# The y halves of a fused attention, expert and gated-MLP kernel: scaled in place, their sums and low halves on GpSimd, with the fetches of the dense weights in another place

## The chip, the cores and the metric

The kernel runs on one core of a Trainium2 chip. The metric is the device time of one execution in microseconds (us). The kernel before took 1469.22 us as the median of three runs (1468.58 to 1472.0). The execution that the profiler recorded took 1465.18 us, of which the trace spans 1463.4 us.

## The reference

Three stages follow one another on 4608 tokens of width 512:

```
attention, 8 x 8 heads, 576 tokens, 64 wide, 32 memory slots:
    a   = softmax(phi over tokens);  k_m = a^T k;  v_m = a^T v
    x   = softmax(q k_m^T / 8) v_m                     -> [4608, 512]
experts (8, capacity 576 each), from all gate logits sorted:
    out[tokens of e] = max(x[tokens of e] @ w1[e], 0) @ w2[e]
                       w1[e]: 512 x 1024, w2[e]: 1024 x 512
gated MLP:
    h   = out @ w_in                                   (512 x 2048)
    out = (h * clip(h + 3, 0, 6) / 6) @ w_out          (2048 x 512)
```

All of it is float32 for the caller. The kernel multiplies in pairs of 16-bit halves: a float32 tile is scaled by a power of two, its high half is the float16 rounding, its low half is the scaled tile minus the high half. A product then takes three matmuls (high by high, high by low, low by high).

## The kernel before, in words

**Stages.** Attention and routing take roughly the first 210 us. The tiles of x are then written to DRAM (`xd<-xs`, through SyncE's queue). From there the work goes by expert, k = 0 to 7. The tokens of an expert are gathered from `xd` by indirect DMAs that GpSimd issues (`h<-xd,ix` for expert 0, `xg<-xd,ix` for the others), transposed on TensorE (`xp`) and split into halves (`xt`). L1(k) is 192 matmuls `p<-xt,w` of 128x288, whose 16 results are taken out by ScalarE (`h<-p`) and VectorE; L2(k) is 192 matmuls `p<-h,w`, whose 8 results ScalarE writes to the y tiles (`y<-p`), with a maximum by VectorE (`ym<-y`).

**Weights.** `weights()` at L1026 runs over T = 0 to 15, where T = 2k is w1 and T = 2k+1 is w2 of expert k. For each it issues four indirect gathers on GpSimd (`wst<-in_moe_w_dram,ei`), squares each on ScalarE (`wscr<-wst`, with a sum), derives a scale (a small matmul `amx<-ident,s_..`, then VectorE), and converts in eight steps: the high halves on ScalarE (`w<-wst,s`), the low halves on VectorE, or for three of the eight on GpSimd while T is 1 to 3.

**The y split.** `ysplit(k)` at L1499 turns the output of expert k into seven pairs of halves, three of blocks of y and four of sums of blocks (a Strassen-like scheme). Before, VectorE makes the four sums and the seven low halves, and ScalarE the seven high halves; the scale `sy` is applied in each of the fourteen steps. A ninth split takes the tokens left over.

**The dense weights.** w_in and w_out are fetched in 32 blocks of 512 KB (`dst`), by SyncE's queue (`dload`, L1212; the fetch itself is at L74 and L76), and converted by VectorE, ScalarE and GpSimd (`cv`, `cva`, `wga`, `wgb`, `wo`), w_in by way of DRAM (`wid`, `ws`). `dense_max`, `dense`, `turn` and `dense_piece` (L1229 on) run this work.

**Units.** Nine units then multiply the split y by the dense weights (`pq`, `pr`), apply the gate (`h`, on ScalarE, VectorE and GpSimd) and multiply by w_out (`acc`). The sequence on TensorE is L1(0), L2(0), L1(1), L2(1), unit 0, unit 1, L1(2), L2(2), L1(3), L2(3), unit 2, and so on, to units 6, 7 and 8.

**What sets the order.** Every engine works through its own instructions in the order in which they were written. That order comes from a model of the clock that runs while the kernel is built: each engine has an object (`A_` ScalarE, `V_` VectorE, `G_` GpSimd) with a modelled time `.t`, and generators yield the modelled time, and the engine, at which they want to go on. `spawn(task, lim)` starts such a generator as a task of its own. On the chip only semaphores and the order in each engine's queue count; the modelled delays exist there only as positions in the queues. Nearly every instruction has one line in the profile, L568, that of the engine objects' call; matmuls are L622 and the transposes L627.

Of the kernel before, what the change touches and what calls it, by code (L numbers as in the profile page):

```python
# [12 lines left out]
AF = mybir.ActivationFunctionType  # L13
OP = mybir.AluOpType
# [5 lines left out]
def attn_moe_kernel(ctx: ExitStack, tc: tile.TileContext, q, k, v, phi, w_gate, w1, w2, w_in, w_out, out):  # L20
    nc = tc.nc
# [535 lines left out]
    CK = Clock()  # L557
# [53 lines left out]
    def spawn(gen, lim=0.0, first=False):  # L611
        t = [CK.now, lim, gen, None]
        CK.tasks.insert(0 if first else len(CK.tasks), t)
# [413 lines left out]
    def weights():  # L1027
        for T in range(2 * E):
            k, which = divmod(T, 2)
            while k not in EIX:  # L1030
                yield CK.now + 0.3
            for c in range(4):
                w_issue(T, c)
                yield CK.now + 0.8, G_
            while not XD[0]:
# [1 line left out]
            sq = rt.tile([128, 4], F32, name="wsq", bufs=2)  # L1037
            for c in range(4):
                st, ready = WST[T, c]
                yield ready, A_  # L1040
                scr = wk.tile([128, 1024], BF16, name="wscr")
                A_.activation(scr, st, AF.Square, accum_out=sq[:, c:c + 1])
                yield (CK.now + 3.0, A_) if k > 3 else A_.t + (0.3 if T else -0.1)
# [169 lines left out]
    def dload(which, j):  # L1213
        tag = spare(1)
        BUSY.add(tag)
        DN[0] += 1
        st = wk.tile([128, 1024], I32, name="dst", tag=tag)
        dense_fetch(st, 16 * which + j)
        return tag, st, dma(1.5)

    EM = []
# [6 lines left out]

    def dense_max():  # L1229
        yield from dense_scale(0)  # L1230
        while not GI[0]:
            yield CK.now + 0.5
        ld = {}
        for n in range(ND[0], 32):
            which, j = divmod(n, 16)
            for i in range(n, min(32, n + 2)):
                while i == n and i not in ld and not spare(1):
                    yield CK.now + 0.3
                if i not in ld and spare(1):
                    ld[i] = dload(*divmod(i, 16))  # L1240
            done, DLD[n], ready = ld[n]
            yield ready, V_
            dense_abs(V_, n)
            yield V_.t
            BUSY.remove(done)
            if j == 15:
                yield from dense_scale(which)
# [5 lines left out]
    WG, WA, WX, NWS, CUR = set(), {}, {}, [0], [0]  # L1253

    def dense():
        while not GI[0]:
            yield CK.now + 0.5
        for which, j in PO:
            while not (SDR[which] and spare(1)):
                yield CK.now + 0.2  # L1260
            spawn(dense_piece(which, j, *dload(which, j)), 0.1)
            yield CK.now

    TURN = [0.0]

    def turn():
        while CK.now < TURN[0] or V_.t > CK.now + 0.05:
            yield max(TURN[0], CK.now + 0.05)
        TURN[0] = CK.now + (1.15 if NB[0] == 4 else 0.85)

    def dense_piece(which, j, done, st, ready):
        yield ready, V_
# [101 lines left out]
    def x_tiles(n):  # L1374
        for _ in range(n):
            if XN[0] == 2 * NT:
                break
            t, g = divmod(XN[0], 2)
            XN[0] += 1
            if g == 0:  # L1380
                XC[:] = [[False]]
                XC.append(bank(XC[0]))
            x_mm(t, ps, XC[1], g)
            CK.now += 0.435
            if g:
                x_ev(t)
                A_.t = max(A_.t, CK.now) + 0.5
                XC[0][0] = True
                XDT[0] = dma(0.73, A_.t)
            XD[0] = XN[0] == 2 * NT  # L1390

    HT, HD, YS, YD = {}, {}, {}, {}
# [105 lines left out]
    def ysplit(k):  # L1498
# [36 lines left out]
            YD[k][0] += 1  # L1535
        else:
            V_.memset(iv[:, 3:4], 1.0)
        t1, t2 = ya[:, :, 0:256], ya[:, :, 256:512]
        u1, u2 = yb[:, :, 0:256], yb[:, :, 256:512]
        ST[k] = [slot(7 * (k % 2) + i, [128, 2, 2, 256], F16, f"st{i}_") for i in range(7)]  # L1540
        nl = [0]
        x1, x2 = (slot(14 + i, [128, 2, 256], F32, f"sx{i}_") for i in range(2))
        V_.tensor_tensor(x1, t2, u2, op=OP.add)
        r1 = V_.t + HOP
        yield V_.t + 0.5, V_
        V_.tensor_tensor(x2, x1, t1, op=OP.subtract)
        r2 = V_.t + HOP
        yield V_.t + 0.5, V_
        V_.tensor_tensor(t2, t1, t2, op=OP.subtract)
        r3 = V_.t + HOP  # L1550
        for i, src, r in ((A11, t1, 0.0), (A12, u1, 0.0), (A22, u2, 0.0), (S1Y, x1, r1), (S2Y, x2, r2), (S3Y, t2, r3),
                          (S4Y, x1, 0.0)):
            if i == S4Y:
                V_.tensor_tensor(x1, u1, x2, op=OP.subtract)
                r = V_.t + HOP
            yield (max(r, CK.now + (0.9 if k == 2 else 2.0)), A_) if k > 1 else (max(r, CK.now + 2.0 * k), A_)
            A_.activation(ST[k][i][:, 0], src, AF.Copy, scale=s)

            def low(t=ST[k][i], src=src):
                yield (A_.t + HOP, V_) if k > 1 else A_.t + HOP  # L1560
                V_.scalar_tensor_tensor(t[:, 1], src, s, t[:, 0], op0=OP.mult, op1=OP.subtract)
                nl[0] += 1
            spawn(low(), 0.8)
            while i in (S1Y, S4Y) and nl[0] < (4, 7)[i == S4Y]:
                yield CK.now + 0.1
        YR[k] = True

    INV, SY = {}, {}
# [232 lines left out]
```

## Time and profile before

| | |
|---|---|
| median of three runs | 1469.22 us |
| profiled execution | 1465.18 us |
| its span in the trace | 1463.4 us |
| TensorE matmul (PE) | 1335.5 us, 91% of the span |
| VectorE (DVE) | 949.7 us, 65% |
| ScalarE (ACT) | 818.9 us, 56% |
| GpSimd (POOL) | 484.6 us, 33% |

The busy times are sums over an execution whose stages differ. In the stretch from 326 to 480 us, which holds the conversion of the dense weights beside expert 1 and the first units, VectorE is busy for nine tenths of the time; from 1002 us on it is busy for less than half.

### The profile page before, as it was taken

The page shows a single profiled execution, that of the slowest core. Times are in us where ns is not written, and L with a number is a line of the kernel's source. Part 1 is how long each engine was busy: PE and PEld are TensorE (multiplying, and loading weights), DVE is VectorE, ACT ScalarE, POOL GpSimd, SP SyncE. Part 2 cuts the span into 40 slices and gives each one's busy share as a digit, 9 for nine tenths or more (in the row PEclk, how much of TensorE's full clock was granted, in tenths as well). Part 3 has the DMA queues.
Part 4 walks back from the last instruction along what each step waited for, and adds up shares of the span by engine and source line. Part 5 has one row for each costly group of instructions (what it writes and reads, how often), then busy time and mean ns, then how long its engine had stood idle before and what let it go on. Part 6 is the DMA issues. An engine that isn't in the chain of part 4 may idle for free.

```text
span 1463.4 us, 27894 instructions
## 1 busy us (share of the span) xinstructions
PE 1335.5 (91%) x11132; PEld 1001.6 (68%) x11132; DVE 949.7 (65%) x2232; ACT 818.9 (56%) x1560; POOL 484.6 (33%) x530
## 2 busy tenths in 40 slices
PE   4778886987999999989899999999999999999998
PEld 3667665866765667877568767876786687666664
DVE  4687975778898888885875687476246424435322
ACT  3667655468687455554654565465437524545543
POOL 5775312145353343302332323323212211232323
PEclk9989997899999999999999999999999999999999
DMA  9984487446773353313332333234223202243321
GB/s 296 309 273 144 158 263 247 145 142 240 248 236 150 109 183 109 104 60 113 109 133 88 119 105 134 91 109 147 81 66 119 101 30 75 81 144 116 107 99 54
DMA packets 83490, 206.29 MB, mean 141 GB/s; under 512 B 11040, under 2 KB 41760, under 8 KB 83360
## 3 DMA queue, kind: packets, MB, share of 16 engines
q1 hardware_dynamic: 68192, 151.55, 30.6%
q0 software_dynamic: 15168, 52.96, 11.1%
q8 instruction: 87, 1.43, 0.4%
q14 instruction: 43, 0.35, 0.1%
HBM read 177.23 MB, written 27.26 MB: 140 GB/s over the span
## 4 chain that ended last, share of the span: by engine, by line
PE 56%; DVE 6%; issue 5%; ACT 2%; DMA 1%; POOL 1%; POOLq 0%; SPq 0%; ACTq 0%
PE acc L622 21%; PE p L622 16%; PE pq L622 10%; PE pr L622 8%; DVE h L568 1%; ACT h L568 1%; DMA wst<-in_moe_w_dram,ei 1%; PE xp L627 1%; DVE w L568 1%; DVE B L568 0%; DVE C L568 0%; PE rtp L838 0%; POOL h L568 0%; DMA ws<-wid 0%; POOL out_dram L568 0%
## 5 line engine op out<-in xcount | busy, mean ns | idle before, releaser
L622 PE MATMUL acc<-wo,h 128*128 128x512 f16 x1728 | 425.0, 380 | 0.3 <-DVE wo L568 0.2
L622 PEld LDWEIGHTS <-w 128*128 128x128 f16 x3072 | 338.2, 122 | 70.8 <-DVE w L568 8.1
L622 PEld LDWEIGHTS <-ws 128*128 128x128 f16 x3024 | 292.2, 98 | 109.8 <-issue 24.4
L568 POOL TENSOR_TENSOR h<-h,h 128x512 f16<-128x512 f32 x144 | 176.6, 1232 | 425.1 <-ACT h L568 300.5
L622 PEld LDWEIGHTS <-h 128*128 128x128 f16 x1728 | 166.3, 98 | 138.7 <-issue 2.3
L622 PE MATMUL p<-h,w 128*128 128x288 f16 x1536 | 206.2, 290 | 10.9 <-DVE w L568 3.9
L622 PE MATMUL p<-xt,w 128*128 128x288 f16 x1536 | 209.3, 291 | 7.3 <-POOL w L568 2.2
L568 ACT ACTIVATE h<-h,half_c,inv 128x512 f32<-128x512 f32 x144 | 116.5, 811 | 175.4 <-DVE h L568 147.3
L568 DVE SCALAR_TENSOR_TENSOR h<-h,h 128x512 f32<-128x512 f32 x144 | 102.4, 713 | 69.8 <-ACT h L568 69.5
L568 ACT ACTIVATE h<-pq,swv 128x256 f32<-128x256 f32 x216 | 101.4, 470 | 63.7 <-PE pq L622 60.4
L568 POOL DMA_INDIRECT wst<-in_moe_w_dram,ei x64 | 65.2, 1018 | 190.7 <-ACT y L568 50.5
L568 ACT ACTIVATE h<-p 128x288 f16<-128x288 f32 x128 | 52.3, 409 | 127.5 <-PE p L622 126.0
L568 DVE SCALAR_TENSOR_TENSOR h<-pr,swv,h 128x256 f32<-128x256 f32 x144 | 69.1, 480 | 84.1 <-PE pr L622 78.1
L568 DVE SCALAR_TENSOR_TENSOR h<-p,h 128x288 f16<-128x288 f32 x128 | 57.5, 453 | 67.9 <-ACT h L568 64.6
L568 DVE SCALAR_TENSOR_TENSOR w<-wst,s,w 128x512 f16<-128x512 f32 x119 | 97.3, 825 | 1.1 <-ACT w L568 1.1
L568 ACT ACTIVATE h<-h 128x512 f16<-128x512 f32 x144 | 89.4, 621 | 8.3 <-DVE h L568 8.2
L568 ACT ACTIVATE w<-wst,s 128x512 f16<-128x512 f32 x119 | 82.7, 712 | 5.7 <-DVE s L568 5.7
L568 ACT ACTIVATE wscr<-wst 128x1024 bf16<-128x1024 f32 x64 | 67.4, 1053 | 15.3 <-DMA wst<-in_moe_w_dram,ei 14.9
L568 ACT ACTIVATE y<-p 128x288 f32<-128x288 f32 x64 | 25.5, 409 | 87.5 <-PE p L622 79.9
L568 DVE TENSOR_REDUCE ym<-y 128x1 f32<-128x288 f32 (+1 forms) x66 | 30.7, 472 | 62.0 <-ACT y L568 61.7
L568 POOL DMA_INDIRECT xg<-xd,ix x35 | 35.9, 1027 | 102.2 <-DVE ix L568 44.5
L568 POOL DMA_INDIRECT out_dram<-y,ix x36 | 36.7, 1019 | 83.1 <-ACT y L568 79.3
(550 smaller groups left out, 2194.3 us busy)
## 6 DMA issues: line engine op xcount, KB each, us to landing
ws<-wid SPq DMA_DIRECT2D x72, 896.0 KB, 4.6
dst<-in_moe_w_out_dram SPq DMA_DIRECT2D x28, 512.0 KB, 5.3
qt<-in_q_dram SPq DMA_DIRECT2D x8, 1024.0 KB, 13.2
dq<-in_moe_w_in_dram SPq DMA_DIRECT2D x16, 512.0 KB, 4.8
xd<-xs SPq DMA_DIRECT2D x32, 256.0 KB, 5.5
dst<-in_moe_w_in_dram SPq DMA_DIRECT2D x16, 512.0 KB, 4.3
kvt<-in_k_dram SPq DMA_DIRECT2D x7, 1152.0 KB, 11.3
kvt<-in_v_dram SPq DMA_DIRECT2D x7, 1152.0 KB, 12.4
```

The lines of the kernel that those rows point to most:

```text
L568: r = f(*a, **kw)
L622: nc.tensor.matmul(o, l, r, start=start, stop=stop, skip_group_check=more)
L627: nc.tensor.transpose(o, i, idn)
```

## The change

The change has four parts.

1. `ysplit`: VectorE first multiplies y by its scale, in place, in two instructions of 128x1024. The seven high halves stay on ScalarE, as copies without a scale. The four sums and the seven low halves go to GpSimd, as subtractions. Each pair of halves is a task of its own.
2. `dload`: three of the early dense blocks are fetched through GpSimd's queue, where before all were fetched through SyncE's. In the written order they stand behind the gathers of expert 0's tokens.
3. The dense work starts once expert 0's tokens have been asked for (`0 in XI`), where before it waited for a later mark (`GI`); in the stage with `NB == 4` its tasks may run further ahead (0.5 where 0.1 and 0.05 stood, and steps of 0.85 where 1.15 stood).
4. `weights`: the third gather waits in the model for x (`XD`), and for T = 1 to 3 the squares are put 2.5 modelled us later. The modelled landing of the last x tile is put 1.5 us later.

```diff
@@ weights()
             for c in range(4):
+                while c == 2 and not XD[0]:
+                    yield CK.now + 0.1
                 w_issue(T, c)
...
                 st, ready = WST[T, c]
-                yield ready, A_
+                yield ready + (2.5 if 0 < T < 4 else 0.0), A_
                 scr = wk.tile([128, 1024], BF16, name="wscr")
@@ dload()
-        dense_fetch(st, 16 * which + j)
+        dense_fetch(st, 16 * which + j, nc.gpsimd if NEM < DN[0] < NEM + 4 else nc.sync)
@@ dense_max(), dense()
-        while not GI[0]:
-            yield CK.now + 0.5
+        while 0 not in XI:
+            yield CK.now + 0.2
...
-            spawn(dense_piece(which, j, *dload(which, j)), 0.1)
+            spawn(dense_piece(which, j, *dload(which, j)), 0.5 if NB[0] == 4 else 0.1)
@@ turn()
-        while CK.now < TURN[0] or V_.t > CK.now + 0.05:
+        while CK.now < TURN[0] or V_.t > CK.now + (0.5 if NB[0] == 4 else 0.05):
             yield max(TURN[0], CK.now + 0.05)
-        TURN[0] = CK.now + (1.15 if NB[0] == 4 else 0.85)
+        TURN[0] = CK.now + 0.85
@@ x_tiles
-                XDT[0] = dma(0.73, A_.t)
+                XDT[0] = dma(0.73, A_.t) + 1.5
@@ ysplit()
+        for y in (ya, yb):
+            V_.tensor_scalar(y[:, :, 0:512], y[:, :, 0:512], s, None, op0=OP.mult)
+            V_.t -= 0.5
+            yield V_.t + 0.3, V_
...
-        V_.tensor_tensor(x1, t2, u2, op=OP.add)
...
-        V_.tensor_tensor(x2, x1, t1, op=OP.subtract)
...
-        V_.tensor_tensor(t2, t1, t2, op=OP.subtract)
...
-            if i == S4Y:
-                V_.tensor_tensor(x1, u1, x2, op=OP.subtract)
-                r = V_.t + HOP
-            yield (max(r, CK.now + (0.9 if k == 2 else 2.0)), A_) if k > 1 else (max(r, CK.now + 2.0 * k), A_)
-            A_.activation(ST[k][i][:, 0], src, AF.Copy, scale=s)
...
-                V_.scalar_tensor_tensor(t[:, 1], src, s, t[:, 0], op0=OP.mult, op1=OP.subtract)
...
+        def half(i, src, r):
+            yield r, A_
+            A_.activation(ST[k][i][:, 0], src, AF.Copy)
+            yield A_.t + HOP, G_
+            G_.tensor_tensor(ST[k][i][:, 1], src, ST[k][i][:, 0], op=OP.subtract)
+            nl.add(i)
+        r = V_.t + HOP
+        for i, src in ((A11, t1), (A12, u1), (A22, u2)):
+            spawn(half(i, src, r), 0.8)
+            yield CK.now + 0.7, G_
+        for i, o, p, q, op in ((S1Y, x1, t2, u2, OP.add), (S2Y, x2, x1, t1, OP.subtract), (S3Y, t2, t1, t2, OP.subtract),
+                               (S4Y, x1, u1, x2, OP.subtract)):
+            while i == S4Y and S1Y not in nl:
                 yield CK.now + 0.1
+            yield CK.now, G_
+            G_.tensor_tensor(o, p, q, op=op)
+            spawn(half(i, o, G_.t + HOP), 0.8)
+            yield G_.t, G_
+        while len(nl) < 7:
+            yield CK.now + 0.1
```

The model clock turns these edits into other orders on the engines. Three places matter for what follows.

**First place: the dense blocks beside expert 0's tokens.** On SyncE's queue before, the dense blocks (`dst`) stand directly behind the last writes of x (`xd`):

```order
L429 DMA xd<-xs_3441 128x512
L429 DMA xd<-xs_3455 128x512
L429 DMA xd<-xs_3469 128x512
L76 DMA dst<-in_moe_w_out_dram 128x1024 x2
L74 DMA dst<-in_moe_w_in_dram 128x4x256
L76 DMA dst<-in_moe_w_out_dram 128x1024 x3
```

On GpSimd's queue after the change, three blocks stand behind the five gathers of expert 0's tokens (`h<-xd,ix`):

```order
L568 DMA wst_3476<-in_moe_w_dram,ei_3356 128x1024
L568 DMA wst_3486<-in_moe_w_dram,ei_3356 128x1024
L568 DMA h_3507<-xd,ix_3499 128x512 x2
L568 DMA h_3578<-xd,ix_3499 128x512 x2
L568 DMA h_3581<-xd,ix_3499 64x512
L76 DMA dst<-in_moe_w_out_dram 128x1024 x2
L74 DMA dst<-in_moe_w_in_dram 128x4x256
L568 DMA wst_3673<-in_moe_w_dram,ei_3356 128x1024
```

Two blocks of w_out and one of w_in have moved from behind the writes of x to behind the gathers, and ahead of expert 0's w2 gathers (`wst_3673`).

**Second place: w2 of expert 1 (T = 3).** On GpSimd before, the fourth gather (`wst_4906`) stands behind two `wgb` steps:

```order
L568 DMA wst_4828<-in_moe_w_dram,ei_4303 128x1024
L568 TENSOR_TENSOR w_3_4800<-wst_4494,w_3_4800 128x512
L568 DMA wst_4841<-in_moe_w_dram,ei_4303 128x1024
L568 TENSOR_TENSOR wgb<-cva,wgb 128x2x256
L568 TENSOR_TENSOR wgb<-cva,wgb 128x256
L568 DMA wst_4906<-in_moe_w_dram,ei_4303 128x1024
```

On GpSimd after the change, the fourth gather (`wst_5208`) stands behind the whole y split of expert 0 (`st__`, `sx__` and `y_`), of which the last rows are:

```order
L568 TENSOR_TENSOR sx__4909<-y_4355,sx__4910 128x512
L568 TENSOR_TENSOR st__4906<-sx__4910,st__4906 128x512
L568 TENSOR_TENSOR st__4907<-y_4349,st__4907 128x512
L568 TENSOR_TENSOR st__4908<-sx__4909,st__4908 128x512
L568 TENSOR_TENSOR wgb<-cva,wgb 128x2x256
L568 TENSOR_TENSOR wgb<-cva,wgb 128x256
L568 DMA wst_5208<-in_moe_w_dram,ei_4314 128x1024
```

Eleven instructions of the y split and two `wga` steps have come ahead of the gather. On ScalarE before, the last square of this weight (`wsq<-wst_4906`) stands ahead of the last three of the 16 evictions of L1(1) (`h_..<-p_..`):

```order
L568 ACTIVATE h_4917<-p_5091 128x288
L568 ACTIVATE wscr,wsq<-wst_4906 128x1024
L568 ACTIVATE h_4917<-p_5112 128x288
L568 ACTIVATE wga<-cva 128x2x256
L568 ACTIVATE h_4973<-p_5133 128x288
L568 ACTIVATE cv<-dst 128x512
L568 ACTIVATE h_4973<-p_5151 128x288
```

On ScalarE after the change, all four squares stand behind the last eviction of L1(1), which is the first row here:

```order
L568 ACTIVATE h_5014<-p_5203 128x288
L568 ACTIVATE sgn<-dst 128x512
L568 ACTIVATE cv<-dst,swv 128x512
L568 ACTIVATE wscr,wsq<-wst_4896 128x1024
L568 ACTIVATE wo_5233<-cv,sd_2752 128x512
L568 ACTIVATE wga<-cva 128x2x256
L568 ACTIVATE wscr,wsq<-wst_4871 128x1024
L568 ACTIVATE wscr,wsq<-wst_4879 128x1024
L568 ACTIVATE cv<-dst 128x512
L568 ACTIVATE wgb<-cva 128x2x256
L568 ACTIVATE wgb<-cva 128x256
L568 ACTIVATE wscr,wsq<-wst_5208 128x1024
```

The squares and seven other steps have moved from beside L1(1) to between L1(1) and L2(1). For T = 2 (w1 of expert 1) the conversions move too: before they begin after the sixth of the eight evictions of L2(0), after the change behind the eighth.

**Third place: w2 of expert 3 (T = 7).** On ScalarE before, the first conversion (`w_0_8839`) stands behind twelve evictions of L1(3), of which the last are:

```order
L568 ACTIVATE st__8705<-y_8203,sy_8569 128x512
L568 ACTIVATE h_8578<-p_8770 128x288
L568 ACTIVATE st__8706<-sx__8710,sy_8569 128x512
L568 ACTIVATE h_8578<-p_8795 128x288
L568 ACTIVATE w_0_8839<-wst_8470,s_3_8754 128x512 x2
```

On ScalarE after the change, it (`w_0_8705`) stands behind the second eviction of L1(3), ahead of the y split:

```order
L568 ACTIVATE y_8379<-p_8560 128x288
L568 ACTIVATE y_8379<-p_8598 128x288
L568 ACTIVATE h_8646<-p_8647 128x288
L568 ACTIVATE h_8646<-p_8662 128x288
L568 ACTIVATE w_0_8705<-wst_8368,s_3_8641 128x512 x2
```

The conversion has moved up by ten evictions.

## Rows read from the trace of the kernel before

**Rows 1.** Windows: stretch, its us, busy us of each engine, PEclk, DMA share, GB/s.

```profile
210.00:262.00 52.00, 37.31 (x461) 27.97 (x457) 33.98 (x112) 31.37 (x40) 11.19 (x11) 0.77 0.73 247
...
326.00:386.00 60.00, 50.98 (x374) 42.67 (x373) 53.11 (x97) 47.87 (x92) 27.13 (x23) 0.91 0.72 239
386.00:480.00 94.00, 88.63 (x613) 59.54 (x612) 86.62 (x163) 71.30 (x133) 38.27 (x31) 0.98 0.56 191
480.00:560.00 80.00, 75.91 (x599) 50.38 (x598) 66.79 (x172) 45.10 (x80) 32.76 (x33) 1.00 0.45 150
560.00:680.00 120.00, 115.39 (x1000) 97.86 (x999) 92.62 (x277) 58.25 (x116) 23.98 (x27) 1.00 0.24 77
680.00:726.00 46.00, 37.06 (x300) 26.29 (x298) 37.55 (x84) 31.55 (x59) 16.68 (x15) 1.00 0.46 153
726.00:1002.00 276.00, 265.82 (x2096) 200.51 (x2095) 193.34 (x475) 151.53 (x288) 81.01 (x75) 1.00 0.33 110
```

**Rows 2.** Waits of TensorE, 326 to 1002: us in total, times, longest.

```profile
PE pr L622 <- DVE h L568: 10.9, 8, 2.6
PE p L622 <- DVE w L568: 4.8, 5, 2.9
...
PE xp L627 <- DVE xt L568: 3.1, 1, 3.1
```

**Rows 3.** Timeline of GpSimd: start, us, instruction, idle before and its releaser.

```profile
246.50 0.96 POOL L568 DMA_INDIRECT h<-xd,ix  x1 [13.03 <-DMA dst<-in_moe_w_out_dram]
```

**Rows 4.** Timeline of SyncE's queue: the dense blocks behind the writes of x.

```profile
239.02 2.46 SPq L76 DMA_DIRECT2D dst<-in_moe_w_out_dram  x2
```

**Rows 5.** Windows, the stretch ahead of the first gather of tokens.

```profile
238.00:246.50 8.50, 2.09 (x44) 1.67 (x44) 5.39 (x20) 5.42 (x10) 0.01 (x1) 0.70 1.05 375
```

**Rows 6.** Timeline of ScalarE: first conversion of T = 2, last eviction of L2(0).

```profile
325.12 0.71 ACT L568 ACTIVATE w<-wst,s 128x512 f16<-128x512 f32 x1
...
330.69 0.41 ACT L568 ACTIVATE y<-p 128x288 f32<-128x288 f32 x1
```

**Rows 7.** Timeline of GpSimd: last low half of T = 2.

```profile
336.28 1.17 POOL L568 TENSOR_TENSOR w<-wst,w 128x512 f16<-128x512 f32 x1
```

**Rows 8.** Timeline of TensorE: end of L1(1), first matmuls of L2(1).

```profile
361.28 0.39 PE L722 MATMUL amx<-ident,s_1m 128*128 128x128 f32 x2
364.90 0.66 PE L622 MATMUL p<-h,w 128*128 128x288 f16 x2 [3.24 <-ACT w L568]
```

**Rows 9.** The page, ScalarE's conversions and squares: busy, mean ns, idle before.

```profile
L568 ACT ACTIVATE w<-wst,s 128x512 f16<-128x512 f32 x119 | 82.7, 712 | 5.7 <-DVE s L568 5.7
L568 ACT ACTIVATE wscr<-wst 128x1024 bf16<-128x1024 f32 x64 | 67.4, 1053 | 15.3 <-DMA wst<-in_moe_w_dram,ei 14.9
```

**Rows 10.** Timeline of GpSimd: two gathers of weights that squares wait for.

```profile
520.21 0.94 POOL L568 DMA_INDIRECT wst<-in_moe_w_dram,ei  x1 [0.30 <-issue]
...
676.09 0.94 POOL L568 DMA_INDIRECT wst<-in_moe_w_dram,ei  x1 [50.46 <-ACT y L568]
```

**Rows 11.** Timeline of ScalarE: the squares that wait for these two gathers.

```profile
529.21 1.06 ACT L568 ACTIVATE wscr<-wst 128x1024 bf16<-128x1024 f32 x1 [2.09 <-DMA wst<-in_moe_w_dram,ei]
...
681.50 1.06 ACT L568 ACTIVATE wscr<-wst 128x1024 bf16<-128x1024 f32 x1 [4.90 <-DMA wst<-in_moe_w_dram,ei]
```

**Rows 12.** Groups of VectorE, 341 to 362: a low half and a sum.

```profile
L568 DVE SCALAR_TENSOR_TENSOR st__4932<-y,sy,st__4932 128x512 f16<-128x512 f32 x1 | 0.7, 747 | 0.0
...
L568 DVE TENSOR_TENSOR y<-y 128x512 f32<-128x512 f32 x1 | 0.7, 681 | 0.0
```

**Rows 13.** The page, GpSimd's two-input step of 128x512.

```profile
L568 POOL TENSOR_TENSOR h<-h,h 128x512 f16<-128x512 f32 x144 | 176.6, 1232 | 425.1 <-ACT h L568 300.5
```

**Rows 14.** Timeline of VectorE: the same pair of steps, alone and beside GpSimd.

```profile
361.62 0.87 DVE L568 TENSOR_TENSOR cva<-cva 128x256 f32<-128x256 f32 x2
...
365.94 1.71 DVE L568 TENSOR_TENSOR cva<-cva 128x256 f32<-128x256 f32 x2
```

**Rows 15.** Timeline of GpSimd: its step beside the slower pair.

```profile
366.20 1.17 POOL L568 TENSOR_TENSOR w<-wst,w 128x512 f16<-128x512 f32 x1 [0.73 <-ACT w L568]
```

More of the change, by code (lines that the diff above doesn't have):

```diff
@@ L1255, in dense @@
     def dense():
-        while not GI[0]:
-            yield CK.now + 0.5
+        while 0 not in XI:
+            yield CK.now + 0.2
         for which, j in PO:
@@ L1540, in ysplit @@
         ST[k] = [slot(7 * (k % 2) + i, [128, 2, 2, 256], F16, f"st{i}_") for i in range(7)]
-        nl = [0]
+        nl = set()
         x1, x2 = (slot(14 + i, [128, 2, 256], F32, f"sx{i}_") for i in range(2))
-        V_.tensor_tensor(x1, t2, u2, op=OP.add)
-        r1 = V_.t + HOP
-        yield V_.t + 0.5, V_
-        V_.tensor_tensor(x2, x1, t1, op=OP.subtract)
-        r2 = V_.t + HOP
-        yield V_.t + 0.5, V_
-        V_.tensor_tensor(t2, t1, t2, op=OP.subtract)
-        r3 = V_.t + HOP
-        for i, src, r in ((A11, t1, 0.0), (A12, u1, 0.0), (A22, u2, 0.0), (S1Y, x1, r1), (S2Y, x2, r2), (S3Y, t2, r3),
-                          (S4Y, x1, 0.0)):
-            if i == S4Y:
-                V_.tensor_tensor(x1, u1, x2, op=OP.subtract)
-                r = V_.t + HOP
-            yield (max(r, CK.now + (0.9 if k == 2 else 2.0)), A_) if k > 1 else (max(r, CK.now + 2.0 * k), A_)
-            A_.activation(ST[k][i][:, 0], src, AF.Copy, scale=s)
-            def low(t=ST[k][i], src=src):
-                yield (A_.t + HOP, V_) if k > 1 else A_.t + HOP
-                V_.scalar_tensor_tensor(t[:, 1], src, s, t[:, 0], op0=OP.mult, op1=OP.subtract)
-                nl[0] += 1
-            spawn(low(), 0.8)
-            while i in (S1Y, S4Y) and nl[0] < (4, 7)[i == S4Y]:
-                yield CK.now + 0.1
+        def half(i, src, r):
[11 more added lines that the diff above has]
+            while i == S4Y and S1Y not in nl:
+                yield CK.now + 0.1
+            yield CK.now, G_
[4 more added lines that the diff above has]
+            yield CK.now + 0.1
         YR[k] = True
```

## The prediction

> **What bounds the kernel now.** I read the page first: TensorE is busy for 91% of the span, so the time is TensorE's work plus its idle pieces, and this change touches no matmul. It can win or lose only idle time and clock. The windows by stage [rows 1] show where these lie: TensorE misses 14.7 us of 52 between 210 and 262 (where its clock is at 0.77), 9.0 between 326 and 386, then 5.4, 4.1, 4.6, 8.9 and 10.2, which is 33 us after 386. VectorE is busy for 53.1 of 60 us and 86.6 of 94 us between 326 and 480, GpSimd for 27.1 and 38.3. The waits [rows 2] say who ends TensorE's idle time from 326 on: VectorE, with 10.9 us before `pr` (the gate's `h`), 4.8 before `p` (weight halves) and 3.1 in one wait for `xt`. Then I read the timeline at the three places where the order changes.
>
> **Part 1, the dense blocks behind the token gathers.** The first gather of expert 0's tokens starts at 246.50 [rows 3]; it reads what the last writes of x bring to DRAM. GpSimd is idle for 13.03 us ahead of it; the row names a dense block as the last to come, but the gather reads `xd`, so I take the writes of x as what it really waits for. The dense blocks were issued at 239.02 [rows 4], into a stretch in which the DMA engines are full: share 1.05, 375 GB/s [rows 5]. Two blocks of 0.52 MB at 375 GB/s are 2.8 us of transfer. Without them the writes of x land earlier by up to 2.8 us; at worst by nothing, if the blocks stood behind the writes anyway. I take 2 us, near the upper end, since the engines are full. A loss is bounded at 1 us: the blocks now land later, and all that waits for them is the maximum over w_in and w_out, which has until the end of L1(0). Expert 0's w2 gathers stand behind the three fetches on GpSimd's queue, 3 x 0.9 us by the nearest row of an issue [rows 10]; L1(0), which comes between, hides that. The wait for x ahead of the third gather moves nothing on the queue.
>
> The Trainium skill says that DMAs started from SyncE's and from GpSimd's queue run on the same 16 DMA engines and interleave ("DMA: Bandwidth & Descriptors", section "Issuing engines are not separate DMA queues"). By that, another queue alone would give nothing here; the later place does. No run so far separates the two.
>
> **Part 2, T = 2 (w1 of expert 1).** Before, its first conversion starts at 325.12, after the sixth eviction of L2(0), and the last eviction follows at 330.69 [rows 6]; its last low half ends at 336.28 + 1.17 = 337.45 on GpSimd [rows 7], and only then does L1(1) run. The conversions take 12.3 us, with two evictions of 0.41 among them. Now they begin only behind the last eviction, at 331.1 by the old clock. They take between 9.6 us (without the evictions and with no wait for a result between) and 12.3, so the last low half ends at 340.7 to 343.4, less the 2 us of part 1: 338.7 to 341.4. That is 1.3 to 4.0 us later than 337.45. I take +2, toward the lower end, as GpSimd and VectorE have fewer dense steps between. If part 1 gives its 2.8, and less dense work stands between, it is -1.
>
> **Part 3, T = 3 (w2 of expert 1): the term against the change.** Before, the scale's matmul (`amx`) runs at 361.28, right at the end of L1(1), and L2(1) starts 3.6 us later, after 3.24 us of idle time [rows 8]. Now, behind the last eviction of L1(1), ScalarE has three squares of 1.05 us and seven other steps of about 0.65 us (the conversions' mean of 0.71 [rows 9] is their upper bound) before the fourth square: 3.2 + 4.6 = 7.8 us; then about 1.25 for that square and the reading of its sum, and 0.4 for the eviction ahead and 0.5 for the way to `amx`. So `amx` comes about 10 us after the end of L1(1), and what follows takes its 3.6 us as before. TensorE works in order and has nothing else to do there: +10 us, uncovered. The other chain into the fourth square is of the same length. GpSimd has to do eleven steps of the y split and two `wga` steps, 13 x 1.23 = 16 us [rows 13], inside the 24 us of L1(1), before it issues the fourth gather; the split starts several us into L1(1), so the gather goes out at about its end, and it lands 5.4 to 9.0 us later (676.09 to 681.50, and 520.21 to 529.21 [rows 10, 11]). Bounds: +6 if the dense steps on ScalarE are shorter and the gather lands in 5.4, +13 if it is issued 4 us after the end of L1(1) and takes 9.0. At the start of unit 0 the kernel is then 2 + 10 = 12 us late.
>
> **Part 4, the y split.** VectorE loses seven low halves of 0.747 and four sums of 0.681 us [rows 12]: 7.95 us a split. It gains two scalings of 128x1024. The trace before shows none; as the work of two of the steps above each is 1.36, at the least 0.68 if the step without a second operand runs twice as fast, at the most 1.5, or 2.3 if held up as in [rows 14]. I take 1.36: relief 7.95 - 2.7 = 5.2 us a split, 47 over nine splits. GpSimd gains 11 x 1.232 = 13.6 us a split [rows 13]; at 33% of the span it has the room, but it stands ahead of gathers, as in part 3, and each low half is now later by 0.5 us. ScalarE's copies keep their length. For TensorE the relief counts only where VectorE is late.
>
> **Part 5, the payback after 386.** The dense conversions have mostly been written ahead of unit 0, where half of them stood beside it, and VectorE is relieved. Between 386 and 480 there are 5.4 us of idle time and 2% of clock, 1.9 us: I take -5 of 7.3. Between 480 and 560: -2.5 of 4.1. Between 560 and 680 the longest wait is one of 2.9 us for a weight half of T = 7 [rows 2], whose conversion now stands ten evictions earlier: -3.5 of 4.6. Between 680 and 726 the waits for `h` and the 3.1 us for `xt` fall into the y split of expert 3 and the transposes of the next, both earlier now: -4.5 of 8.9. Between 726 and 1002, two more splits: -5.5 of 10.2. Together -21. New waits, for y halves behind GpSimd's gate steps: +1. Bounds: -10 (half of it) to -30.
>
> **Sum.** 12 - 21 + 1 = -8 us. Against the profiled execution, 1465.18 - 8 = 1457.2. That execution lies 4.0 us under the median of the runs, so the forecast for a median is 1469.2 - 8 = 1461 us.
>
> **Rivals.**
> *A, the wait ahead of L2(1) is not paid back.* Mechanism: T = 3's gather behind the y split on GpSimd, its squares behind L1(1) on ScalarE. Price: +13 there, +4 for T = 2, and half the payback, -10 with +1 for new waits: +8, 1477 us. It decides from the point at which the fourth square starts over 12 us after the end of L1(1) while the units still wait for `h`. For it: the order is certain, and nothing covers it. Against it: 33 us of idle time follow, most of it ended by VectorE.
> *B, GpSimd's steps hold VectorE up.* The same pair of VectorE steps takes 0.87 us alone and 1.71 beside a GpSimd step of 1.17 [rows 14, 15]. Eleven GpSimd steps a split, each holding VectorE by 0.84, are 9.2 us, more than the relief of 5.2. Then the waits for `h` and `xt` (14 us) stay: -21 becomes -7, and 12 - 7 + 1 = +6, 1475 us. Against it: that row is one meeting, and VectorE is idle for a third of the span, so many of GpSimd's steps will meet none of its steps.
> The Trainium skill says that VectorE and GpSimd share a port pair of SBUF, which one of them holds for a whole instruction when VectorE has two inputs in SBUF or is in a two-port mode ("SBUF — State Buffer", section "🔬 SBUF: two separate sides"). The rows agree: 0.84 more beside a step of 1.17. It also advises VectorE for two-input elementwise work, GpSimd being about twice as slow ("GPSIMD Engine Reference", section "4.1 Engine selection"); here 1.232 against 0.681 is 1.8 times. By these rules the move to GpSimd would not pay, which is this rival.
> *C, the wait ahead of L2(1) stays small,* because L1(1) itself is late and the squares' data come early: 2 - 21 + 1 = -18, 1451 us. Against it: the squares stand behind the last eviction in the queue, whatever the data do.
> *D, part 1 does nothing,* because the writes of x and not the blocks fill the engines: 2 us more, 1463.
>
> **How the numbers follow.** Forecast 0.55 (its own range 1454 to 1467), A 0.17, B 0.10, C 0.12, D 0.06. About 0.3% (4.4 us) is what a measurement of this kernel can tell from no change: faster is below 1464.8, slower above 1473.6. The forecast gives 0.40 faster, 0.12 same, 0.03 slower; A 0.02 same, 0.15 slower; B 0.04 same, 0.06 slower; C 0.12 faster; D 0.04 faster, 0.02 same. Sums: 0.56, 0.20, 0.24. The range goes from 1447, which takes in C with some of the greatest payback, to 1477, the price of A.
>
> **What would show it.** Part 1: the first gather of tokens starts near 244.5. Part 2: the first eviction of L1(1) comes 2 us later than before. Part 3: TensorE is idle for about 13 us ahead of L2(1), where it was 3.2, released by a weight half, with a clock at half speed behind it; 5 us or less would make C right. Part 4: VectorE busy about 47 us less, GpSimd 122 more; a scaling near 1.4 us. If VectorE's busy time falls by under 20, it is B. Part 5: less than 14 us of TensorE's waits left between unit 0 and 1002; if more than 23 are left, the payback was mis-sized, and the time is 1469 or above.

## The result and the profile after

The changed kernel takes 1489.52 us (median of four runs, 1487.05 to 1491.2) against 1468.9 us before: a ratio of 1.0135, 95% interval 1.0114 to 1.0155. It is 20.6 us slower, where I forecast 8 us faster, and it lies outside the range. The profiled execution took 1491.2 us, 1.7 above its median, where that of before lay 4.0 under its own; so the two traces differ by 26 us, where the medians differ by 20.6: some 5 us of what the traces show is no effect of the change.

The windows of the changed kernel, as in [rows 1] (stretch, its us, busy us of each engine, PEclk, DMA share, GB/s):

```profile
210.00:262.00 52.00, 39.72 (x501) 29.69 (x498) 35.55 (x116) 32.40 (x42) 13.34 (x14) 0.79 0.73 239
...
326.00:386.00 60.00, 35.75 (x239) 29.47 (x238) 53.59 (x104) 45.92 (x89) 37.46 (x34) 0.75 0.78 252
386.00:480.00 94.00, 89.41 (x673) 63.21 (x672) 77.98 (x159) 63.91 (x121) 44.90 (x39) 0.99 0.47 162
480.00:560.00 80.00, 73.97 (x559) 48.86 (x558) 63.57 (x163) 43.33 (x78) 33.16 (x32) 0.96 0.45 153
560.00:680.00 120.00, 113.98 (x947) 94.19 (x945) 95.83 (x256) 61.70 (x123) 43.06 (x41) 0.99 0.28 92
680.00:726.00 46.00, 40.74 (x352) 31.87 (x351) 31.23 (x65) 24.23 (x48) 17.33 (x16) 0.99 0.31 104
726.00:1002.00 276.00, 267.37 (x2077) 200.73 (x2077) 186.75 (x439) 150.07 (x285) 103.11 (x95) 0.99 0.32 107
1002.00:1440.00 438.00, 429.38 (x3058) 307.16 (x3057) 180.92 (x332) 214.25 (x399) 162.38 (x150) 0.99 0.29 97
```

Between 326 and 386 TensorE misses 24.3 us, where it missed 9.0, and its clock falls to 0.75. The stretches behind have hardly become fuller, against my forecast: from 386 to 1002 TensorE misses 30.5 us where it missed 33.2, with 12.1 in place of 8.7 between 480 and 680, and beyond 1002 it misses 8.6 us where it missed 1.5. Fixed windows mix stages once a kernel is late, so I set the same events side by side (ScalarE's evictions in the timelines; the change to the trace of before, in us, minus is earlier). The columns to the right are runs told of below. The first row is the drift between executions: up to the last write of x the order is the same in all of them on ScalarE, VectorE, GpSimd and SyncE's queue, and still that write is issued at 238.60 us before and 0.6 us earlier to 4.1 later in the others.

| event | changed | e1 | e2 | e4 | e8 | e11 |
|---|---|---|---|---|---|---|
| last write of x issued | +2.2 | +0.4 | +3.3 | +0.8 | -0.6 | +4.1 |
| last eviction of L2(0) | -0.7 | +0.3 | -0.5 | -2.1 | -3.6 | +2.4 |
| first eviction of L1(1) | +7.2 | +0.3 | +7.3 | +2.5 | +1.0 | +3.7 |
| last eviction of L1(1) | +7.9 | +0.5 | +9.0 | +5.1 | +6.3 | +3.8 |
| first eviction of L2(1) | +18.7 | +0.3 | +4.3 | +4.1 | +5.3 | +4.2 |
| first eviction of L1(2) | +21.2 | -1.4 | +2.3 | +3.2 | +1.7 | +0.2 |
| first eviction of L1(4) | +22.2 | +1.6 | -3.5 | +5.8 | -11.4 | -2.3 |
| first eviction of L1(5) | +19.5 | +3.3 | -6.4 | +7.6 | -13.8 | -5.2 |
| first eviction of L1(6) | +25.2 | +9.3 | -9.2 | +13.5 | -15.8 | -7.9 |
| first eviction of L1(7) | +25.7 | +9.8 | -8.4 | +14.1 | -15.3 | -7.2 |

Two things are seen in the first column. Some 19 us are lost by the start of L2(1), of which 2.2 are the drift. After that nothing comes back on balance, and two more losses, of 2.5 and 5.7 us, stand between L2(1) and L1(6). (The columns are of profiled executions, which lie up to 6.4 us from the medians given below.)

**The first loss.** The timeline of TensorE in the changed kernel, the end of the wait ahead of L2(1) (start, us, instruction, idle before and its releaser), against [rows 8]:

```profile
379.54 0.79 PE L722 MATMUL amx<-ident,s_1m 128*128 128x128 f32 x2 [10.17 <-DVE s_1m L568]
383.54 0.66 PE L622 MATMUL p<-h,w 128*128 128x288 f16 x2 [3.21 <-ACT w L568]
```

TensorE waits 10.17 us for the scale of w2 of expert 1, and 3.21 more for its first half, where it waited only 3.24 in all. The timeline of ScalarE shows why: the last eviction of L1(1), then the first and the last of the four squares. Between these ScalarE pauses only for 0.23 us, so it is its own queue that holds the last square back.

```profile
369.41 0.41 ACT L568 ACTIVATE h<-p 128x288 f16<-128x288 f32 x1 [0.25 <-PE p L622]
...
371.32 1.04 ACT L568 ACTIVATE wscr<-wst 128x1024 bf16<-128x1024 f32 x1
...
377.04 1.04 ACT L568 ACTIVATE wscr<-wst 128x1024 bf16<-128x1024 f32 x1
```

GpSimd issues the gather that this last square reads only after the y split, 1.5 us before that eviction. Its data come in time, as the square starts without a wait:

```profile
363.06 1.34 POOL L568 TENSOR_TENSOR st__4908<-sx__4909,st__4908 128x512 f16<-128x512 f32 x1 [0.27 <-ACT st__4908 L568]
366.00 1.80 POOL L568 TENSOR_TENSOR wgb<-cva,wgb 128x512 f16<-128x512 f32 x2 [1.60 <-ACT wgb L568]
367.95 0.96 POOL L568 DMA_INDIRECT wst<-in_moe_w_dram,ei  x1
```

**What did not come back.** The busy times of the changed kernel's page:

```profile
PE 1345.0 (90%) x11132; PEld 1008.0 (68%) x11132; DVE 940.4 (63%) x2155; ACT 814.5 (55%) x1556; POOL 605.8 (41%) x631
```

GpSimd is 121 us more busy, as forecast (122). VectorE is only 9.3 us less busy (it was 949.7). Added up from the timelines, its y split took 87.0 us in 99 steps and now takes 16.5 in 18. So 70.5 us of work left VectorE, and its other work has become longer. Taken by itself, as the time in which at least one other step runs, that work was 874.6 us and is now 926.3, some 52 us more. (The remaining 9 us are overlap: in the trace, steps that follow each other overlap a little, and there was more of this between y steps and others before.) The longest single case is here, VectorE's timeline first (the low half of a weight takes 7.32 us where [rows 12] show 0.75 for a step of this size), then GpSimd's at the same time, six y steps without a pause:

```profile
720.78 0.47 DVE L568 SCALAR_TENSOR_TENSOR h<-pq,swv,h 128x256 f32<-128x256 f32 x1
721.18 7.32 DVE L568 SCALAR_TENSOR_TENSOR w<-wst,s,w 128x512 f16<-128x512 f32 x1
728.42 0.47 DVE L568 SCALAR_TENSOR_TENSOR h<-pr,swv,h 128x256 f32<-128x256 f32 x1
```

```profile
720.91 1.16 POOL L568 TENSOR_TENSOR st__9644<-y,st__9644 128x512 f16<-128x512 f32 x1
722.03 1.27 POOL L568 TENSOR_TENSOR sx__9651<-y,y 128x512 f32<-128x512 f32 x1
723.25 1.15 POOL L568 TENSOR_TENSOR st__9645<-y,st__9645 128x512 f16<-128x512 f32 x1
724.36 1.25 POOL L568 TENSOR_TENSOR sx__9652<-sx__9651,y 128x512 f32<-128x512 f32 x1
725.58 1.14 POOL L568 TENSOR_TENSOR st__9646<-y,st__9646 128x512 f16<-128x512 f32 x1
726.69 1.25 POOL L568 TENSOR_TENSOR y<-y 128x512 f32<-128x512 f32 x1
```

VectorE's step ends 0.56 us after GpSimd's last one. Elsewhere it is a chain of small routing steps, each of which takes about as long as one step of GpSimd. Here is VectorE's timeline around 1007; GpSimd runs gate steps (`h`) and y steps in turn from 1005.12 to 1009.74, of 1.16 to 1.28 us each:

```profile
1005.53 2.03 DVE L568 SCALAR_TENSOR_TENSOR scn<-scn,off,G 128x36 f32<-128x36 f32 x2
1007.60 1.08 DVE L568 TENSOR_TENSOR sl<-scn 128x36 f32<-128x36 f32 x1
1008.72 1.06 DVE L568 TENSOR_SCALAR sl<-sl 128x36 f32<-128x36 f32 x1
```

The last two of them in the kernel before:

```profile
986.26 0.20 DVE L568 TENSOR_TENSOR sl<-scn 128x36 f32<-128x36 f32 x1
986.49 0.18 DVE L568 TENSOR_SCALAR sl<-sl 128x36 f32<-128x36 f32 x1
```

Behind these stand steps for which TensorE waits; its timeline has one long wait behind the step of 7.32 us and one behind the chain:

```profile
729.01 0.17 PE L858 MATMUL rtp<-FL,onesb 128*128 128x8 bf16 x1 [5.96 <-DVE FL L568]
...
1014.87 1.01 PE L622 MATMUL pr<-st__11348,ws 128*128 128x256 f16 x4 [6.07 <-DVE h L568]
```

The waits of the changed kernel from 410 to 1060 (us in total, times, longest):

```profile
PE pr L622 <- DVE h L568: 9.7, 5, 6.1
PE rtp L858 <- DVE FL L568: 6.5, 2, 6.0
PE rtp L927 <- DVE tot L568: 4.9, 3, 2.5
PE xp L627 <- DVE xt L568: 3.5, 1, 3.5
PE rtp L991 <- DVE OH L568: 3.4, 2, 2.7
```

The waits for `h` are about as long in total as before (9.7 us, where the same stretch had 10.6), but one has 6.1 us, and the three of the routing (`rtp`), for which TensorE did not wait before, are 14.8 us.

### The profile page after: what moved, and what is told of

Same layout as the page of the kernel before. It is cut to its first block, busy times and chain, and to the rows that moved or that the text cites. A ratio compares the mean times of both kernels' runs of the same rounds, so it can differ in the third digit from the quotient of the medians.

```text
span 1489.4 us, 27900 instructions
## 1 busy us (share of the span) xinstructions
PE 1345.0 (90%) x11132; PEld 1008.0 (68%) x11132; DVE 940.4 (63%) x2155; ACT 814.5 (55%) x1556; POOL 605.8 (41%) x631
## 4 chain that ended last, share of the span: by engine, by line
PE 71%; DVE 18%; ACT 5%; issue 3%; DMA 2%; POOL 1%; SPq 0%; POOLq 0%; DVEq 0%; ACTq 0%
PE acc L622 22%; PE p L622 21%; PE pq L622 11%; PE pr L622 8%; DVE h L568 2%; DVE w L568 2%; PE xa L419 2%; PE kvp L190 2%; ACT h L568 1%; PE xp L627 1%; DVE ql L329 1%; DVE C L568 1%; DVE cva L568 1%; ACT A L169 1%; DMA dst<-in_moe_w_in_dram 1%
## 5 line engine op out<-in xcount | busy, mean ns | idle before, releaser
L622 PE MATMUL acc<-wo,h 128*128 128x512 f16 x1728 | 429.6, 382 | 0.0
L568 POOL TENSOR_TENSOR h<-h,h 128x512 f16<-128x512 f32 x144 | 172.0, 1201 | 358.1 <-ACT h L568 250.4
L568 DVE SCALAR_TENSOR_TENSOR h<-h,h 128x512 f32<-128x512 f32 x144 | 117.8, 820 | 77.1 <-ACT h L568 76.2
L568 DVE SCALAR_TENSOR_TENSOR w<-wst,s,w 128x512 f16<-128x512 f32 x119 | 110.1, 928 | 2.4 <-ACT w L568 2.4
L568 ACT ACTIVATE h<-h 128x512 f16<-128x512 f32 x144 | 89.3, 622 | 14.0 <-DVE h L568 13.8
L568 DVE SCALAR_TENSOR_TENSOR h<-pq,swv,h 128x256 f32<-128x256 f32 x72 | 34.7, 481 | 53.2 <-PE pq L622 52.5
```

What stands on the lines that cost most here:

```text
L568: r = f(*a, **kw)
L622: nc.tensor.matmul(o, l, r, start=start, stop=stop, skip_group_check=more)
```

## The experiments

From the trace of the changed kernel my theory was: the order of T = 2 and T = 3 loses 19 us, and the payback fails because steps of GpSimd hold VectorE up (theory 1, later H). The rivals were that the relief counts and only the order hides it (2), that the y split costs in itself (3), and that it costs through GpSimd's queue, by late gathers and late halves (Q). All ratios are to the kernel before, run on the same chip. The experiments ran on three chips, where its median was 1467.44 to 1469.41 us, so a difference between two runs can be off by 2 us.

**e1: the y split alone.** The kernel before with the new body of `ysplit`:

```diff
-            A_.activation(ST[k][i][:, 0], src, AF.Copy, scale=s)
+            A_.activation(ST[k][i][:, 0], src, AF.Copy)
...
-                V_.scalar_tensor_tensor(t[:, 1], src, s, t[:, 0], op0=OP.mult, op1=OP.subtract)
+            G_.tensor_tensor(ST[k][i][:, 1], src, ST[k][i][:, 0], op=OP.subtract)
...
```

> The kernel before with the new y split alone (scaled in place, sums and low halves on GpSimd); T = 2 and T = 3 keep the old order on ScalarE. Theory 1 (the loss is the order of T = 2 and T = 3, 8.6 + 10.7 us at the start of unit 0 in the trace after; the relief of VectorE is eaten because GpSimd's steps hold VectorE's): 1465 to 1473 us, VectorE's busy time within 15 us of before. Theory 2 (the relief counts, and only the order hides it): 1450 to 1460, VectorE 40 us less busy. Theory 3 (the y split on GpSimd is itself the loss): 1480 or more.

Measured: 1475.63 us, ratio 1.0049 (1.0028 to 1.0070): slower, by about 7 us, and 2.6 us above what I expected of theory 1. VectorE's busy time fell by 18.7 us. T = 2 and T = 3 keep their place and cost nothing (+0.3 at L2(1)); the kernel is 1.4 us ahead at L1(2), and loses 11 us between there and L1(7). That is neither theory 1's range nor theory 3's; theory 2 is out. VectorE's work outside the y split takes 916.8 us, 42 more than before.

**e2: everything but the y split.** The changed kernel with the old body of `ysplit`:

```diff
-            yield A_.t + HOP, G_
-            G_.tensor_tensor(ST[k][i][:, 1], src, ST[k][i][:, 0], op=OP.subtract)
...
+                V_.scalar_tensor_tensor(t[:, 1], src, s, t[:, 0], op0=OP.mult, op1=OP.subtract)
...
```

> The changed kernel with the y split of before: dense blocks behind the gathers, deeper queues, 2.5 in weights; T = 2 is converted behind the last eviction of L2(0), T = 3 stands nearly where it stood. Theory 1: L1(1) starts 7 us late as in the changed kernel, L2(1) waits about 4 us, 1470 to 1478 us. Theory 2: the same start, 1470 to 1478. Theory 3: 1465 to 1470, as everything but the y split is neutral.

Measured: 1453.51 us, ratio 0.9900 (0.9873 to 0.9926): 16 us faster than before, which none of the three theories gave. The rest of the change is good, and the y split takes 36 us from it (34 by the ratios). L1(1) starts 7.3 us late here too, of which 3.3 are the drift, so the lateness of T = 2 is not the y split's; but of the other 4.0 us 1.0 is left at L2(1), and nothing at L1(2).

**e4: without the late squares.** The changed kernel with

```diff
-                yield ready + (2.5 if 0 < T < 4 else 0.0), A_
+                yield ready, A_
```

> The changed kernel without the 2.5 in weights: the squares of T = 3 stand beside L1(1) again and its fourth gather ahead of most of the y split; T = 2 starts one eviction earlier. Theory 1: the wait of 13 us ahead of L2(1) falls to 3 to 5, 1474 to 1481 us. Theory 2: the same. Theory 3: 1486 to 1490, since the time lost there only moves on.

Measured: 1479.38 us, ratio 1.0071 (1.0046 to 1.0095), 10.1 us less than the changed kernel and within the range of theories 1 and 2. The wait ahead of L2(1) is gone (+4.1 there). What is left is the y split: from +3.2 at L1(2) to +14.1 at L1(7). TensorE has one wait of 7.94 us behind the same routing chain, seen in its timeline:

```profile
1002.77 1.44 PE L622 MATMUL pr<-st__11321,ws 128*128 128x256 f16 x6 [7.94 <-DVE h L568]
```

**e5: pauses between GpSimd's steps.** The changed kernel with

```diff
             G_.tensor_tensor(ST[k][i][:, 1], src, ST[k][i][:, 0], op=OP.subtract)
+            G_.memset(gap, 0.0)
...
             G_.tensor_tensor(o, p, q, op=op)
+            G_.memset(gap, 0.0)
```

> The changed kernel with a tiny memset behind each of GpSimd's y steps, the same order on every engine otherwise. If a run of GpSimd steps that follow each other without a pause keeps a waiting VectorE step out (7.32 us in one step at 721 in the trace after), and a pause of 0.1 us lets it in: no VectorE step of 128x512 longer than 2.5 us, VectorE 10 to 20 us less busy, 1476 to 1485 us. If each GpSimd step holds VectorE for itself, pause or not: VectorE's busy time within 5 us of the changed kernel's, 1488 to 1492.

Measured: 1490.12 us, ratio 1.0149 (1.0117 to 1.0182), VectorE busy for 939.3 us: as the changed kernel. One sign of the first reading came true: no step of 128x512 takes over 2.2 us. But other steps took the place of the one of 7.32 us, the longest a routing step of 128x1 (`fp`) with 4.02 us, which outlasts three y steps of GpSimd and the memsets of 0.1 us between them. So such a pause does not let VectorE in. For the time as a whole this run is a weaker test, since the order on the other engines did not stay: the memsets count in the model, and ScalarE's and VectorE's orders differ from 354 us on.

**e8: GpSimd as busy, but only writing.** From e4:

```diff
-            G_.tensor_tensor(ST[k][i][:, 1], src, ST[k][i][:, 0], op=OP.subtract)
+            G_.memset(ST[k][i][:, 1], 0.0)
+            nc.gpsimd.memset(ST[k][i][:, 1], 0.0)
...
-            G_.tensor_tensor(o, p, q, op=op)
+            G_.memset(o, 0.0)
+            nc.gpsimd.memset(o, 0.0)
```

> The changed kernel without the 2.5, and each of GpSimd's y steps replaced by two memsets of its output (about 0.52 us each by the memsets of 64x512 in the trace before): GpSimd is as busy, at the same places, but reads nothing there. The sums and low halves are left out, so they are zero. Theory H (GpSimd's reading steps hold VectorE's): VectorE's longest weight and routing steps fall under 2.5 us, VectorE 25 to 40 us less busy than before, 1448 to 1462 us. Theory Q (the y split costs through GpSimd's queue: gathers and gate steps stand behind it, halves come later): as without the memsets, 1475 to 1483 us.

Measured: 1450.78 us, ratio 0.9892 (0.9870 to 0.9915), 28.6 us less than e4 (26 by the ratios). ScalarE, VectorE, GpSimd and SyncE's queue have their instructions in the same order as in e4. The busy times of e4 and of e8 on their pages:

```profile
PE 1343.4 (91%) x11132; PEld 1005.4 (68%) x11132; DVE 933.7 (63%) x2153; ACT 812.7 (55%) x1558; POOL 610.2 (41%) x630
```

```profile
PE 1334.3 (92%) x11132; PEld 1002.1 (69%) x11132; DVE 890.0 (61%) x2153; ACT 812.5 (56%) x1558; POOL 580.9 (40%) x729
```

With 96 us more on GpSimd than before, where e4 has 126, VectorE's busy time falls by 59.7 us, where it fell by 16.0 in e4; theory H had 25 to 40. Its work outside the y split takes 875.0 us, as before (874.6), where e4 has 919.7. TensorE is idle for 20 us less than in e4, and its own work takes 9.1 us less. The waits of TensorE for `h` in e8, from 410 to 1060, are 3.9 us where e4 has 16.4 (the row of e4, then that of e8):

```profile
PE pr L622 <- DVE h L568: 16.4, 9, 7.9
```

```profile
PE pr L622 <- DVE h L568: 3.9, 7, 2.3
```

Theory Q has two ways left. The memsets are shorter (0.54 us each on average, two for a step of 1.33), and they do not wait for ScalarE's high halves, so GpSimd's queue may run ahead of e4's. The waits say that it gave nothing: from 326 us on ScalarE waits for GpSimd for 11.7 us in both runs, its squares for their gathers for 9.6 and 9.1 us, and the only wait of TensorE for GpSimd is the same, for weight halves (this row stands in both):

```profile
PE p L622 <- POOL w L568: 3.7, 2, 2.9
```

In neither does it wait for a y half. Theory Q is out, theory H holds.

**e3: the new form, on VectorE.** The changed kernel with

```diff
-            yield A_.t + HOP, G_
-            G_.tensor_tensor(ST[k][i][:, 1], src, ST[k][i][:, 0], op=OP.subtract)
+            yield A_.t + HOP, V_
+            V_.tensor_tensor(ST[k][i][:, 1], src, ST[k][i][:, 0], op=OP.subtract)
...
-            G_.tensor_tensor(o, p, q, op=op)
+            V_.tensor_tensor(o, p, q, op=op)
```

> The changed kernel with its new y split (scaled in place, tasks apart), but the sums and low halves on VectorE. Theory H or Q (it is GpSimd that costs): 1450 to 1458 us, as with the old y split (1453.5), although VectorE is some 80 us more busy than its work in the changed kernel alone would be. If the form of the split costs (the scaling ahead, the tasks): 1465 or more.

Measured: 1464.87 us, ratio 0.9984 (0.9969 to 0.9999). It lies between the two expectations: 14.5 us better than on GpSimd (e4; L2(1) starts 4.1 us late in both), 11.4 worse than the old form (e2). VectorE is 7.2 us more busy than in e2, for two scalings more a split; why this costs 11 us is not settled.

**e12: only the sums on GpSimd.** From e3, the four sums of each split back on `G_`:

```diff
-            yield CK.now, V_
-            V_.tensor_tensor(o, p, q, op=op)
-            spawn(half(i, o, V_.t + HOP), 0.8)
-            yield V_.t, V_
+            yield CK.now, G_
+            G_.tensor_tensor(o, p, q, op=op)
+            spawn(half(i, o, G_.t + HOP), 0.8)
+            yield G_.t, G_
```

> The run with the new y split on VectorE (1464.9 us), with the four sums back on GpSimd: 4 of the 11 steps, about 44 us more on GpSimd. If each reading step of GpSimd costs its share by holding VectorE, less the VectorE time that it saves (0.68 each): 1463 to 1472 us, VectorE's other steps 10 to 20 us longer in sum. If the hold counts only in long unbroken runs of GpSimd steps: 1457 to 1462, since VectorE is relieved by 24 us.

Measured: 1466.76 us, ratio 0.9987 (0.9975 to 1.0000); 36 steps of 55 us in all on GpSimd. No gain for 36 steps taken off VectorE: at 0.68 each [rows 12] they were 24 us, but its busy time falls by 1.8 us against e3 (957.6 to 955.8), so its other steps take some 22 us more (step by step, with what overlaps counted twice, 7 us in the low halves and 18 outside the split). That is the first reading, a little beyond its bound. The order of other steps moved too, so the unchanged time is not the effect of the hold alone.

**e6 and e7: which part of e2 gains.** e6 is e2 without the 2.5 (the same line as in e4), e7 is e2 with

```diff
-        dense_fetch(st, 16 * which + j, nc.gpsimd if NEM < DN[0] < NEM + 4 else nc.sync)
+        dense_fetch(st, 16 * which + j)
```

> All of the change but the y split and the 2.5 in weights: T = 2 is converted an eviction earlier than with it. If T = 2's lateness (L1(1) 7 us late in the trace) still counts at the end: 1447 to 1452. If it is taken up by waits that follow: 1452 to 1456 us. It also stands against the run without the 2.5 (1479.4), from which only the y split differs.

> All of the change but the y split, with the three dense blocks on SyncE's queue again. If the blocks behind the gathers gain nothing (the first gather started at 248.6 and 248.9 in the runs with them, 246.5 and 246.8 in those without): within 3 us of 1453.5. If they gain 2 us, as I forecast: 1455 to 1457, with the first gather 2 us later.

Measured: 1454.38 us (ratio 0.9914, 0.9894 to 0.9934) and 1454.17 us (0.9921, 0.9901 to 0.9942): neither part moves the time. In e7 the first token gather starts at 246.87, in e2 at 248.94 and in e6 at 247.60, but most of that is the drift: counted from the issue of the last write of x it is 7.5, 7.0 and 7.1 us. The dense blocks held it up by about half a us.

**e11: the deeper queues alone.** The kernel before with

```diff
-            spawn(dense_piece(which, j, *dload(which, j)), 0.1)
+            spawn(dense_piece(which, j, *dload(which, j)), 0.5 if NB[0] == 4 else 0.1)
...
-        while CK.now < TURN[0] or V_.t > CK.now + 0.05:
+        while CK.now < TURN[0] or V_.t > CK.now + (0.5 if NB[0] == 4 else 0.05):
             yield max(TURN[0], CK.now + 0.05)
-        TURN[0] = CK.now + (1.15 if NB[0] == 4 else 0.85)
+        TURN[0] = CK.now + 0.85
```

> The kernel before with only the deeper queues of the dense conversion (the numbers in dense and turn): weights from T = 4 on stand where they stand in the run without the y split, T = 2 and T = 3 as before. If the 14 us of the run without the y split come from the queues: 1450 to 1457 us. If they come from the late squares, the model's x time or the dense start: 1464 to 1470.

Measured: 1451.62 us, ratio 0.9887 (0.9864 to 0.9911). Three lines give the whole gain, and this version beats both kernels. In its order the conversions from T = 4 on stand where they stand in e2. Why that shortens the waits was not tested. The waits of TensorE from 410 to 1060, where these three rows had 10.6, 3.3 and 3.1 us before:

```profile
PE pr L622 <- DVE h L568: 6.5, 10, 1.5
PE xp L627 <- issue: 2.0, 1, 2.0
PE xp L627 <- DVE xt L568: 2.0, 1, 2.0
```

## Why the prediction was wrong

The sum failed in its payback: from the start of L2(1) on I had -20 us (-21 + 1), and the traces show +7. Parts 1 to 3 had +12 there and came to some 16 without the drift.

- **Part 1 was mis-sized.** I forecast the first gather 2 us earlier. In the changed kernel it starts 2.1 us later, with another releaser:

```profile
248.62 1.07 POOL L568 DMA_INDIRECT h<-xd,ix  x1 [12.86 <-DVE TH L568]
```

  These 2.1 us are the drift, since the last write of x is already issued 2.2 us later. Counted from that issue, the gather starts 7.5 to 8.0 us later in the four traces with the blocks on SyncE's queue, and 6.8 to 7.8 in the eight with them behind the gathers: 0.7 us on average, a third of what I took. Rival D was nearly right. I had taken the full DMA engines [rows 5] for the blocks' doing.
- **Part 2 was mis-sized.** T = 2 costs 8.6 us at L1(1) (-0.7 to +7.9), where I took 4 (2 with part 1's gain; bounds 3.3 to 6.0). The conversions begin at 331.35, as I had it, but take 13.2 us to the last low half, where I took 9.6 to 12.3: dense steps lie among them, and that last half alone takes 2.18 us beside a step of GpSimd. Ahead of it something did give the 2 us, and more, that I had put down to part 1: without the drift L2(0) ends 2.9 us earlier, and 2.8 in e7, where the blocks are on SyncE's queue again. Which edit does it was not tested. The lateness did not count in the end: e6, where L1(1) starts 3.2 us late, and e2, with 7.3, are equal (1.3 and 4.0 us without the drift).
- **Part 3 was right in its size.** The wait ahead of L2(1) is 10.17 + 3.21 = 13.4 us (forecast: about 13), the loss 10.8 us (forecast: 10); e4 gives 10.1 back. It needs both edits, the 2.5 and the y split on GpSimd: without the y split the 2.5 costs nothing (e2 against e6). Of my two chains, ScalarE's queue came last.
- **Part 4 was the step that failed.** I forecast a relief of VectorE of 5.2 us a split, 47 over nine splits. Its y work fell by 70.5 us (a scaling takes 0.74 us when nothing holds it, little over half of what I took, and the old steps were being held too), but its busy time fell by 9.3 us, since its other work became 52 us longer beside GpSimd's steps. Rival B had the mechanism and the test, under 20 us less busy time; I gave it a chance of 0.10 and the price of one brief meeting of 0.84 us [rows 14, 15], and did not see that one VectorE step can wait through six steps of GpSimd, nor that chains of small routing steps pay 1.1 us each. The trace before had a longer meeting, which I did not use: a step of VectorE beside two gate steps of GpSimd, 3.23 us long. VectorE's row comes first, then GpSimd's.

```profile
996.98 3.23 DVE L568 SCALAR_TENSOR_TENSOR st__12931<-sx__12932,sy,st__12931 128x512 f16<-128x512 f32 x1 [0.46 <-ACT st__12931 L568]
```

```profile
997.38 2.28 POOL L568 TENSOR_TENSOR h<-h,h 128x512 f16<-128x512 f32 x2
```

- **Part 5 was wrong in its cause.** Of the 21 us of payback nothing came in the changed kernel. The part due to the deeper queues is real, 15 to 17 us (e11, e2), as long as the y split stays on VectorE. VectorE's relief is worth little even where GpSimd does not hold it up: e8, with VectorE busy for 58 us less than e6, is 3.6 us faster, which measurements hardly tell apart. GpSimd's y split costs 7 us on the kernel before (e1), but 25 beside the deeper queues (e4 against e6; 23 by the ratios) and, with the late squares, 36 (changed kernel against e2). Of the 25 us, 14.5 go when the same steps run on VectorE (e4 against e3). Why the cost grows with the queues, and why the new form on VectorE costs 11 us, stays open.

On the mechanism: the Trainium skill says that VectorE and GpSimd share a port pair, held for a whole instruction by the one that starts first, when VectorE has two inputs in SBUF or runs in a two-port mode, the first only against a GpSimd step that reads SBUF ("SBUF — State Buffer", section "🔬 SBUF: two separate sides"). e8 agrees with the last point: a two-input step of VectorE (`sl<-scn`) takes its 0.20 us beside a memset of GpSimd, while the one-input step behind it (`sl<-sl`, 0.18 us alone) ends only with the next memset. Whether that step runs in a two-port mode the trace does not show. VectorE's timeline comes first, then GpSimd's.

```profile
971.23 0.20 DVE L568 TENSOR_TENSOR sl<-scn 128x36 f32<-128x36 f32 x1
971.45 0.60 DVE L568 TENSOR_SCALAR sl<-sl 128x36 f32<-128x36 f32 x1
```

```profile
970.91 0.53 POOL L568 MEMSET y<- 128x512 f32 x1
971.49 0.53 POOL L1567 MEMSET y<- 128x512 f32 x1
```

In the changed kernel VectorE waited through six GpSimd steps in a row, 7.32 us, not through one.

## What to carry to other kernels

A step moved from VectorE to GpSimd was not off VectorE here: 131 us of GpSimd steps with two inputs made VectorE's other work 52 us longer, two fifths of their time. So price GpSimd's time as time that VectorE may lose, and look at which chains on VectorE stand beside it. A difference of busy times between two traces shows this at once, before any wait is read. And an edit to a written order that costs nothing alone (late squares) can cost 10 us beside another that moves the same gather: try such edits one at a time. The order ahead of an edit tells how far two traces have drifted apart; take that off before comparing times of events.

## What the runs showed of the hardware

In the changed kernel a VectorE step that takes 0.74 us elsewhere took 7.32 us beside six GpSimd steps in a row, and in e4 one of 0.46 took 5.23 beside four. In e5 a pause of 0.1 us between GpSimd's steps, filled by a memset, did not let VectorE in (4.02 us across three steps). Steps with one input of 36 columns were held as well (1.06 us for 0.18). Beside GpSimd steps that only write (e8), VectorE's work outside the y split took as long as before, 875.0 us. A float32 scaling of 128x1024 from SBUF to SBUF took 0.74 us, as long as a two-input step of half that size (0.75 us [rows 12]).
